# A fused attention recurrence and MLP: order of TensorE's work, masks and turned keys of the later chunks

## The chip, the cores and the metric

The kernel runs on one core of a Trainium2 chip. The metric is device time in microseconds (us) of one execution. The core has five engines with queues of their own, which run beside each other: TensorE (PE: matmuls and transposes; PEld is its loading of weights), VectorE (DVE), ScalarE (ACT), GpSimd (POOL) and SyncE (SP, which here only issues DMAs). Matmuls write into PSUM, everything else lives in SBUF or in DRAM.

## The reference

Two blocks, one behind the other. The first is a gated linear recurrence over 768 positions, for each of 4 batches and 8 heads with 48 elements each; the second an MLP with silu on the 3072 tokens x 384 features that come out of it.

```python
state = zeros(B, H, 48, 48)
for t in range(768):
    state = alpha[:, :, t, :, None] * state + einsum('bhd,bhe->bhde', k[:, :, t], v[:, :, t])
    y[:, :, t] = einsum('bhd,bhde->bhe', q[:, :, t], state)
x = y.transpose(0, 2, 1, 3).reshape(3072, 384)
h = x @ w_in                      # 384 x 2048
out = (h / (1 + exp(-h))) @ w_out # 2048 x 384
```

All is in fp32. The weights come as 64-bit floats and are rounded in the kernel.

## The kernel before

**Chunks.** The 768 positions are cut into 6 chunks of 128 for each of 4 batches: 24 chunks, numbered n = 4 * ci + b (`ci` the place in time, `b` the batch). Heads go in 4 pairs. For a chunk the recurrence becomes a few matmuls. These are its stages:

- `products` (L694): alpha, k and q are turned so that the features lie on partitions; for the first 8 chunks by TensorE with an identity, for the later ones by VectorE (`turned`, L692). A scan along the chunk (L717) gives `u`, the running products of alpha; `least` (L720) is the product over the whole chunk; `kp` is k times `u`.
- `quotient` (L736): a second scan (L746) gives `p`, and q times it (L751) is `qp`, in the same buffer.
- `scores` (L773): kp times qp into two PSUM tiles (`ps_a`), one for each head of the pairs. They are brought into `g` in SBUF with everything above the diagonal set to zero. The state of this batch is then scaled by `least` on ScalarE (L817).
- `values` (L822): `g` times v and qp times the state into PSUM, copied into `xt` (L842), the input of the MLP.
- `states` (L843): k (`kn`, with tokens on partitions) times v, added to the state (L859). The last four chunks have no such stage.

**The MLP in pieces.** Four chunks are a group of 512 tokens, six groups in all. The work of a group is cut into pieces that are woven between the stages of later chunks. `enter_plain` (L888) does the first layer of groups 0 and 1 with plain matmuls and a silu on ScalarE (L900). `enter` (L908) does that of the other groups by a scheme with fewer matmuls and more additions: 20 block products, whose operands are sums of blocks of x (`sums_x`, into `xc`) and of the weights (`sums_w`, into `wx` and `w_in`), and whose results are put together by ScalarE (copies L927, silu L932) and VectorE (L935, L1010). `leave` (L1012) does the second layer in 7 block products of 16 matmul records each (128 x 192), with VectorE's subtractions (L1024), and stores the output tiles `o` (L1033, L1036). `audit` (L653) reads alpha and the weights again and reduces them (L681) for a check of whether the fast way holds; a general way stands behind a branch and is not taken here.

**Order.** A loop over 25 steps with 4 slots runs a chunk's stages, and after each slot `fill` (L1157) releases those pieces whose due time has come; `marks` (L1143) set the due times of the groups. The framework's scheduler may move instructions within an engine's queue as it sees fit, by its own costs, unless an instruction is kept in program order. At step 8 `settle` (L1145) frees the buffers of the first stage and opens those of the second (`late`). From then on every PE instruction is kept in program order, by the small class `pe` that wraps matmul and transpose.

**The later chunks (n >= 8).** In one step: `land` and `scores` of the chunk before, `products`, `quotient`, then `values` and `states` of the chunk before and `flip`. The buffer `p` is one of two in turn. After `flip` the loads of the next chunk are issued on SP's queue: four DMAs each for alpha (`at`), k (`kt`) and q (`qt`), and those of v (`vn`).

- *Mask.* `scores` writes only the part of a chunk that is needed, with the key halves of the second two pairs exchanged. ScalarE copies it into one fixed tile `decayed` (L799 twice, L802 four times a chunk), and GpSimd sets the part above the diagonal to zero in four selects (L806). The part that is never written was set to zero once.
- *Turned keys.* `flip` (L753) and `land` (L765) bring `kp` to `kn`, tokens on partitions: VectorE transposes 32 x 32 blocks (L761), one DMA writes them to DRAM (`flips`, L763), four DMAs read them back in the other order (L771). This is done for chunks 8 to 19.

**Stores.** `o` has three buffers. The stores of the first five groups (40) go out on GpSimd's queue, the last eight on SP's.

Of the kernel before, what the change touches and what calls it, by code (L numbers as in the profile page):

```python
# [355 lines left out]
def quotients(  # L356
# [19 lines left out]
    nc = tc.nc  # L376
    dve, act, gps = nc.vector, nc.scalar, nc.gpsimd

    late = {}

    def in_order(ins):

        return tc.keep_in_program_order(ins) if late else ins

    class pe:
        @staticmethod
        def matmul(*args, **kw):
            in_order(nc.tensor.matmul(*args, **kw))  # L388

        @staticmethod  # L390
        def transpose(*args):
            in_order(nc.tensor.transpose(*args))

    B, H, S, D = q.shape
# [27 lines left out]
    gpool = pool("gpool", 6)  # L422
    opool = pool("opool", 3)
    rpool = pool("rpool")
    dram = pool("dram", 2, bass.MemoryType.DRAM)
    upool = pool("upool")
# [107 lines left out]
    def turns(x, n):  # L534

        return x[(n + 1) % 2]

# [8 lines left out]


    decayed = fix.tile([128, 2 * NP * C], F32, name="g")
    low, high = slice(0, CH), slice(CH, C)
    earlier, later = [(low, 0), (high, 1)], [(low, 1), (high, 0)]  # L550
    ones = consts.tile([128, 1], F32, name="ones")
    gps.memset(ones, 1.0)

# [129 lines left out]

    xts, xcs = {}, {}

# [8 lines left out]
    def products(n):  # L694

        c = ctxs[n]
        sg = seg[0 if late else n % 2]
        ps = {}

        for name in ("a", "k", "q"):  # L700
            if n >= NA:
                if name == "a":
                    turned(c[name], tokens(sg))
                continue
            if n < GB and name != "a":

                at = "kq".index(name)
                ps[name] = (bank(at) if n == 1 else out_bank(at, 512)).rearrange("p (j c) -> p j c", c=C)
            else:
                ps[name] = ps_attn()  # L710
            for j in range(NP):
                pe.transpose(ps[name][:, j, :], c[name][:, 2 * j : 2 * j + 2, :], ident)
            if name == "a":
                act.copy(tokens(sg), ps[name])  # L714
        end = NP * W
        u = upool.tile([128, end + 1], F32, name="u")
        dve.tensor_tensor_scan(u[:, end - 1 :: -1], sg[:, end:0:-1], one[:, end:0:-1],  # L717
                               0.0, ALU.mult, ALU.add)

        dve.tensor_single_scalar(least[:, n, :], u[:, 0:end:W], 2.0**-64, ALU.max)  # L720
        kp = c["kp"] = turns(kps, n) if n < NA else kps[0]
        ut = tokens(u)
        if n >= NA:
            ps["k"] = late["turn"].tile([128, NP, C], F32, name="turn")
            turned(c["k"], ps["k"])
        if n < NA:
            dve.tensor_tensor(kp, ps["k"], ut, ALU.mult)
            quotient(n, sg, ps["q"])
            return
        j = NP // 2  # L730
        dve.tensor_tensor(kp[:, 0:j], ps["k"][:, 0:j], ut[:, 0:j], ALU.mult)
        k, ut = [x[:, j:].rearrange("p j (e c) -> p j e c", e=2) for x in (ps["k"], ut)]
        dve.tensor_tensor(kp[:, j:].rearrange("p j (e c) -> p j e c", e=2)[:, :, ::-1], k, ut, ALU.mult)
        c["sg"] = sg

    def quotient(n, sg=None, q=None):  # L736
# [7 lines left out]
        dve.reciprocal(iv[:, 0:end:W], least[:, n, :])  # L744
        p = turns(qps if n < NA else [qps[0], late["p"]], n)
        dve.tensor_tensor_scan(p[:, 0:end], sg[:, 0:end], iv[:, 0:end], 0.0, ALU.mult, ALU.add)  # L746
# [5 lines left out]

    def flip(n):  # L753

        c = ctxs[n]
        if n < NA or c["ci"] == NCH - 1:
            return
        t = late["turn"].tile([128, NP, C], F32, name="turn").rearrange("p c (j d) -> p c j d", j=NP)  # L760
        dve.transpose(t, c["kp"].rearrange("p j (c i) -> p c j i", i=32))  # L761
        c["flip"] = dram.tile([128, NP * C], F32, name="flips")
        nc.sync.dma_start(c["flip"], t.rearrange("p c j d -> p (c j d)"))  # L763

    def land(n):  # L765
        c = ctxs[n]
        if "flip" in c:
            c["kn"] = work.tile([128, NP, C], F32, name="kn")
            x = c.pop("flip").rearrange("(r d) (i x) -> i d r x", r=4, i=4)
            for i in range(4):  # L770
                nc.sync.dma_start(c["kn"][32 * i : 32 * i + 32], x[i])  # L771

    def scores(n):  # L773
        c = ctxs[n]
        ci, b = c["ci"], c["b"]
        ps = [ps_attn() for _ in range(2)]

        for j in (0, 2, 1, 3):  # L780
            for e in range(2 if n >= NA else 1):
                for u in range(2):
# [4 lines left out]
                              start=True, stop=True)  # L787
        g = decayed.rearrange("p (u j c) -> p u j c", u=2, j=NP)
        swapped = decayed.rearrange("p (o u j c) -> p o u j c", o=2, u=2, j=NP // 2)
        c["g"] = (lambda u, j: g[:, u, j, :]) if n < NA else (  # L790
            lambda u, j: swapped[:, j // 2, u, j % 2, :])
        for u in range(2 if n < NA else 0):
            act.copy(g[:, u], ps[u])
            gps.affine_select(g[:, u], g[:, u], pattern=[[0, NP], [1, C]], compare_op=ALU.is_ge,
                              fill=0.0, base=0, channel_multiplier=-1)
        if n >= NA:
            ps = [x.rearrange("p (o j) c -> p o j c", o=2) for x in ps]
            for u in range(2):
                act.copy(swapped[:, :, u, :, CH:], ps[u][:, :, :, CH:])  # L799
            for r, o in earlier:  # L800
                for u in range(2):
                    act.copy(swapped[r, o, u, :, 0:CH], ps[u][r, o, :, 0:CH])  # L802
            for at, half in ((CH, later), (0, earlier)):
                for r, o in half:
                    x = swapped[r, o].rearrange("p u j c -> p (u j) c")[:, :, at : at + CH]
                    gps.affine_select(x, x, pattern=[[0, NP], [1, CH]],  # L806
                                      compare_op=ALU.is_ge, fill=0.0, base=0, channel_multiplier=-1)
        if n < NA and ci < NCH - 1:
            ps_k = ps_attn()
# [12 lines left out]
    def values(n):  # L822

        c = ctxs[n]
        ci, b, g, qp = c["ci"], c["b"], c.pop("g"), c["qp"]
        vn = c["v"].rearrange("p (j u) d -> p j (u d)", u=2)
        s = st[b].rearrange("p j u e -> p j (u e)")
        py = ps_attn()
        todo = [(3 * j + i, vn[:, j, at : at + 32], g(u, j))
                for j in range(NP) for i, at, u in ((0, 0, 0), (1, 32, 0), (2, 80, 1))]  # L830
        todo += [(3 * j + 1, vn[:, j, 48:80], g(1, j)) for j in range(NP)]
        if ci > 0:
# [10 lines left out]
    def states(n):  # L843
        c = ctxs.pop(n)
        ci, b, vn = c["ci"], c["b"], c["v"]
        if ci < NCH - 1:

            ps = ps_attn()
            for j in range(NP):
                for i in range(4):  # L850
                    r = slice(32 * i, 32 * i + 32)
                    kn = c["kn"][:, j, r] if n < NA else c["kn"][:, i, 32 * j : 32 * j + 32]
                    pe.matmul(ps[r, j, 0:D], lhsT=kn, rhs=vn[:, 2 * j + i // 2, 0:D],
                              start=True, stop=True)
# [14 lines left out]
    def sums_x(grp):  # L869
        xcs[grp] = late["xc"].tile([128, len(SUMS_X), TB], F32, name="xc")  # L870
        for to, sa, a, sb, b in SUMS_X:
            tc.keep_in_program_order(
                combine(block_x(grp, to), sa, block_x(grp, a), sb, block_x(grp, b)))
        yield
# [137 lines left out]
    def leave(grp, h):  # L1012
# [14 lines left out]
        def store(m, c, x, y=None):  # L1027
# [6 lines left out]
            r = b * S + ci * C  # L1034

            (gps if grp < NG - 1 else nc.sync).dma_start(out[r : r + C, c * HO : (c + 1) * HO], o)  # L1036

# [104 lines left out]

    marks = [2 * SLOTS + 2] + [(GB * i + 2 * GB) * SLOTS + 3 for i in range(len(phases))]  # L1143

    def settle():  # L1145
# [4 lines left out]
        quads = pool("quads")  # L1150
        late["p"] = pool("p").tile([128, NP * W + 1], F32, name="p")
        late["quads"] = {name: quads.tile([128, 32 + 4 * NP * D], F32, name=f"{name}t") for name in "akq"}
# [23 lines left out]
    for step in range(STEPS):  # L1176
# [6 lines left out]
        elif step >= NA:  # L1183
            stages = [[(land, 1), (scores, 1)], [(products, 0)], [(quotient, 0)],
                      [(values, 1), (states, 1), (flip, 0)]]
        for slot, group in enumerate(stages):
            for stage, lag in group:
# [6 lines left out]
                if stage is states and n + 1 + NIN < NA:  # L1194
                    load(n + 1 + NIN)
                if stage is flip and n + 1 < NT:
                    load(n + 1)
                if stage is states and n + NV < NT:
                    load_v(n + NV)
            if step * SLOTS + slot == (NA + 1) * SLOTS - 1:  # L1200
                x = decayed.rearrange("p (o i c) -> p o i c", o=2, c=C)
                for r, o in later:
                    gps.memset(x[r, o, :, 0:CH], 0.0)
            fill(step, slot)
# [22 lines left out]
    ps = ps_attn()[0:1, 0, 0:1]  # L1227
    pe.matmul(ps, lhsT=good, rhs=ones, start=True, stop=True)
    dve.tensor_single_scalar(small, ps, 127.5, ALU.is_ge)
# [62 lines left out]
```

## Time and profile before

| | |
|---|---|
| median of 3 runs | 568.21 us (567.66 to 568.32) |
| the profiled execution | 568.32 us, span 566.6 us, mean granted clock of TensorE 0.993 |
| PE busy | 545.6 us (96%) |
| DVE busy | 444.1 us (78%), 801 instructions |
| ACT busy | 207.7 us (37%) |
| POOL busy | 72.6 us (13%) |
| DMA | 70.13 MB, mean 124 GB/s |

The span is that of the instructions on the core; the execution's time holds 1.7 us more. Busy shares are means over stages with different limits, so the profile is read by stage. Its groups of instructions are given as line, engine, operation, out<-in, number, then busy time in all, mean duration in ns, and idle time of the engine just before them with what ended it. The durations of TensorE's matmuls overlap, so that the distance from start to start in a dense stream says what one costs. A wait is told by the engine that waited and by what released it.

The rows that tell what the parts concerned take:

| row | count | busy us | mean ns |
|---|---|---|---|
| L799 ACT copy g<-ps_a, 128x256 | 32 | 10.2 | 369 |
| L802 ACT copy g<-ps_a, 64x128 | 64 | 13.6 | 262 |
| L793 ACT copy g<-ps_a, 128x512 (first 8 chunks) | 16 | 8.6 | 588 |
| L794 POOL select, 128x512 (first 8 chunks) | 16 | 12.5 | 804 |
| L813 ACT copy kn<-ps_a (first 8 chunks) | 8 | 4.8 | 605 |
| L927 ACT copy g<-ps_m, 128x512 | 64 | 36.6 | 588 |
| L935 DVE g<-ps_m,g, 128x512 | 56 | 37.3 | 682 |
| L1036 POOL issue of stores | 40 | 22.1 | 552 |
| L771 SP issue of kn<-flips | 48 | | 430 (median) |
| L763 SP issue of flips | 12 | | 344 (median) |

### The profile page before, as it was taken

How to read it: one execution, taken by the hardware profiler on the slowest of the kernel's cores; microseconds unless marked ns; L12 is line 12 of the kernel's file. 1: busy time of each engine (PE TensorE's matmuls, PEld its weight loads, DVE VectorE, ACT ScalarE, POOL GpSimd, SP SyncE). 2: the span in 40 equal slices, each digit the busy share in tenths (PEclk: the TensorE clock that was granted, in tenths of full speed). 3: DMA queues.
4: the chain of work that ended last, by engine and by line, in shares of the span. 5: the costliest groups of instructions: out<-in, count | busy, mean ns of one | idle time of the engine just before them, and what ended most of it. 6: DMA issues, size and time to landing. Idle time of an engine off the chain costs nothing. (4 is left out here: it accounts for less than half of the span.)

```text
span 566.6 us, 12602 instructions
## 1 busy us (share of the span) xinstructions
PE 545.6 (96%) x5026; PEld 489.6 (86%) x5026; DVE 444.1 (78%) x801; ACT 207.7 (37%) x466; POOL 72.6 (13%) x146
## 2 busy tenths in 40 slices
PE   6999999999979999999999999999999999999995
PEld 4788887998968989889999989998898999997995
DVE  5997879885957799998997988997993776857531
ACT  3565654313312242353341553442462341422100
POOL 3110111221111020210110212110221000001000
PEclk9999999999997999999999999999999999999999
DMA  9999761233542343345546355455432132333010
GB/s 218 251 270 203 203 182 53 63 104 105 144 125 79 109 124 86 101 115 158 161 124 167 113 167 140 128 159 139 120 104 79 53 101 90 112 104 113 29 31 25
DMA packets 99220, 70.13 MB, mean 124 GB/s; under 512 B 56272, under 2 KB 88656, under 8 KB 99152
## 3 DMA queue, kind: packets, MB, share of 16 engines
q1 hardware_dynamic: 97232, 65.30, 43.3%
q0 software_dynamic: 1920, 3.93, 2.0%
q8 instruction: 41, 0.67, 0.5%
q14 instruction: 27, 0.22, 0.1%
HBM read 61.34 MB, written 7.86 MB: 122 GB/s over the span
## 5 line engine op out<-in xcount | busy, mean ns | idle before, releaser
L388 PE MATMUL ps_o<-w_out,g 128*128 128x192 f32 x768 | 134.6, 329 | 1.6 <-DVE o L1033 1.4
L388 PEld LDWEIGHTS ps_o<-w_out,g 128*128 128x128 f32 x768 | 125.4, 190 | 5.5 <-DVE o L1033 2.5
L388 PE MATMUL ps_m<-xt,w_in 128*128 128x256 f32 x480 | 116.6, 390 | 5.0 <-ACT g L900 3.6
L388 PEld LDWEIGHTS ps_m<-xt,w_in 128*128 128x128 f32 x480 | 90.6, 193 | 19.3 <-ACT g L900 3.9
L388 PE MATMUL ps_o<-wt,g 128*128 128x192 f32 x576 | 99.7, 326 | 0.0
L388 PEld LDWEIGHTS ps_o<-wt,g 128*128 128x128 f32 x576 | 95.1, 190 | 1.6 <-issue 0.2
L388 PE MATMUL ps_m<-xc,w_in 128*128 128x256 f32 x288 | 70.8, 382 | 2.0 <-ACT part L927 1.4
L388 PEld LDWEIGHTS ps_m<-xc,w_in 128*128 128x128 f32 x288 | 53.6, 190 | 9.4 <-ACT part L927 1.7
L681 DVE TENSOR_REDUCE seen<-bits 128x1 f32<-128x384 int32 (+2 forms) x65 | 42.5, 688 | 21.3 <-DMA bits<-in_moe_w_out_dram 20.4
L1024 DVE TENSOR_TENSOR g<-g 128x512 f32<-128x512 f32 x72 | 48.5, 689 | 6.1 <-PE ps_o L388 6.1
L932 ACT ACTIVATE g<-g 128x1024 f32<-128x1024 f32 x32 | 33.3, 1056 | 53.1 <-DVE g L935 52.8
L388 PE MATMUL ps_m<-xc,wx 128*128 128x256 f32 x192 | 50.1, 383 | 0.1
L1036 POOL DMA_DIRECT2D out_dram<-o x40 | 22.1, 552 | 219.1 <-DVE o L1033 130.2
L927 ACT COPY g<-ps_m 128x512 f32<-128x512 f32 x64 | 36.6, 588 | 35.4 <-PE ps_m L388 34.9
L806 POOL TENSOR_SCALAR_AFFINE_SELECT g<-g 64x256 f32<-64x256 f32 x64 | 30.5, 477 | 141.3 <-ACT g L799 124.0
L817 ACT ACTIVATE st<-st,least 128x96 f32<-128x96 f32 x80 | 24.3, 365 | 57.4 <-DVE least L720 57.3
L935 DVE TENSOR_TENSOR g<-ps_m,g 128x512 f32<-128x512 f32 x56 | 37.3, 682 | 3.3 <-PE ps_m L388 3.0
L388 PEld LDWEIGHTS ps_m<-xc,wx 128*128 128x128 f32 x192 | 35.1, 190 | 4.6 <-ACT g L927 0.4
L717 DVE TENSOR_TENSOR_SCAN u<-al,one 128x516 f32<-128x516 f32 x24 | 29.5, 1227 | 9.9 <-ACT al L714 9.5
L692 DVE STREAM_TRANSPOSE al<-at 128x512 f32<-128x512 f32 x16 | 17.8, 1111 | 19.3 <-DMA at<-in_alpha_dram 11.9
L900 ACT ACTIVATE g<-ps_m 128x512 f32<-128x512 f32 x32 | 19.0, 595 | 37.5 <-PE ps_m L388 37.4
L746 DVE TENSOR_TENSOR_SCAN p<-al,inv 128x516 f32<-128x516 f32 x24 | 29.6, 1234 | 0.6
(126 smaller groups left out, 617.3 us busy)
## 6 DMA issues: line engine op xcount, KB each, us to landing
bits<-in_moe_w_in_dram SPq DMA_DIRECT2D x24, 512.0 KB, 4.6
bits<-in_moe_w_out_dram SPq DMA_DIRECT2D x32, 384.0 KB, 3.1
at<-in_alpha_dram SPq DMA_DIRECT2D x64, 96.0 KB, 2.5
kt<-in_k_dram SPq DMA_DIRECT2D x64, 96.0 KB, 2.5
qt<-in_q_dram SPq DMA_DIRECT2D x64, 96.0 KB, 2.5
bits<-in_alpha_dram SPq DMA_DIRECT2D x9, 512.0 KB, 3.9
out_dram<-o POOLq DMA_DIRECT2D x40, 96.0 KB, 2.0
flips<-turn SPq DMA_DIRECT2D x12, 256.0 KB, 2.4
```

The lines of the kernel that those rows point to most:

```text
L388: in_order(nc.tensor.matmul(*args, **kw))
L681: dve.tensor_reduce(seen[kind][which][:, i : i + 1], x, axis=AX, op=op, apply_absolute_value=True))
L717: dve.tensor_tensor_scan(u[:, end - 1 :: -1], sg[:, end:0:-1], one[:, end:0:-1], 0.0, ALU.mult, ALU.add)
L746: dve.tensor_tensor_scan(p[:, 0:end], sg[:, 0:end], iv[:, 0:end], 0.0, ALU.mult, ALU.add)
L806: gps.affine_select(x, x, pattern=[[0, NP], [1, CH]], compare_op=ALU.is_ge, fill=0.0, base=0, channel_multiplier=-1)
L817: act.mul(s[:, j], s[:, j], least[:, n, j : j + 1])
L900: act.activation(gts[grp, h, pair][:, i : i + 2, q % 2, :], ps, AF.Silu)
L927: act.copy(to, ps)
L932: act.activation(x, x, AF.Silu)
L935: dve.tensor_tensor(to, a, b, op)
L1024: dve.tensor_tensor(cells(grp, h, pair, *to), cells(grp, h, pair, *x), cells(grp, h, pair, *y), ALU.subtract)
L1036: (gps if grp < NG - 1 else nc.sync).dma_start(out[r : r + C, c * HO : (c + 1) * HO], o)
```

## The change

- The class `pe` goes; TensorE's instructions, and the sums of x on VectorE, are left to the scheduler throughout.
- Masks of the later chunks: two PSUM tiles are blanked by ScalarE (`blank`, behind `quotient`) before the scores are written into parts of them, and VectorE multiplies each whole tile with a mask of ones and zeros into `g`. The mask is built at the start by GpSimd. `g` is a tile of its own for each chunk (one buffer) in place of `decayed`. The masks of the first eight chunks are made as before.
- Turned keys of chunks 8 to 19: by four TensorE transposes with the identity and one ScalarE copy, as in the first eight chunks, in the stage `scores`. `flip`, `land` and the DRAM tile go.
- `p` has one buffer in the later chunks, and `quotient` and `blank` stand behind `values` and `states`. The loads of the next chunk follow `quotient`.
- All stores go out on SP's queue, `o` has two buffers.
- The due times of the groups come one slot earlier.

```diff
-    class pe:
-        @staticmethod
-        def matmul(*args, **kw):
-            in_order(nc.tensor.matmul(*args, **kw))
-        @staticmethod
-        def transpose(*args):
-            in_order(nc.tensor.transpose(*args))
+    pe, dve, act, gps = nc.tensor, nc.vector, nc.scalar, nc.gpsimd
...
-    opool = pool("opool", 3)
+    opool = pool("opool", 2)
...
+    mask = consts.tile([128, 2, C], F32, name="mask")
+    gps.memset(mask, 1.0)
+    for odd in range(2):
+        for e in range(2):
+            m = mask[CH * e : CH * e + CH, odd, :]
+            gps.affine_select(m, m, pattern=[[1, C]], compare_op=ALU.is_ge, fill=0.0,
+                              base=-CH * (e ^ odd), channel_multiplier=-1)
...
-        p = turns(qps if n < NA else [qps[0], late["p"]], n)
+        p = turns(qps, n)
...
-    def flip(n):
...
-        t = late["turn"].tile([128, NP, C], F32, name="turn").rearrange("p c (j d) -> p c j d", j=NP)
-        dve.transpose(t, c["kp"].rearrange("p j (c i) -> p c j i", i=32))
-        c["flip"] = dram.tile([128, NP * C], F32, name="flips")
-        nc.sync.dma_start(c["flip"], t.rearrange("p c j d -> p (c j d)"))
-    def land(n):
...
-            for i in range(4):
-                nc.sync.dma_start(c["kn"][32 * i : 32 * i + 32], x[i])
+    def blank(n):
+        if n < NA:
+            return
+        ps = ctxs[n]["blank"] = [ps_attn() for _ in range(2)]
+        for t in ps:
+            act.activation(t.rearrange("p j c -> p (j c)"), ident[:, 0:1].to_broadcast([128, 4 * C]),
+                           AF.Copy, scale=0.0)
...
-            for u in range(2):
-                act.copy(swapped[:, :, u, :, CH:], ps[u][:, :, :, CH:])
-            for r, o in earlier:
-                for u in range(2):
-                    act.copy(swapped[r, o, u, :, 0:CH], ps[u][r, o, :, 0:CH])
-            for at, half in ((CH, later), (0, earlier)):
-                for r, o in half:
-                    x = swapped[r, o].rearrange("p u j c -> p (u j) c")[:, :, at : at + CH]
-                    gps.affine_select(x, x, pattern=[[0, NP], [1, CH]],
-                                      compare_op=ALU.is_ge, fill=0.0, base=0, channel_multiplier=-1)
-        if n < NA and ci < NCH - 1:
+            m = mask[:, :, None, :]
+            dve.tensor_tensor(g[:, u].rearrange("p (o j) c -> p o j c", o=2),
+                              ps[u].rearrange("p (o j) c -> p o j c", o=2),
+                              m.to_broadcast([128, 2, NP // 2, C]), ALU.mult)
+        if ci < NCH - 1:
             ps_k = ps_attn()
             for j in range(NP):
                 pe.transpose(ps_k[:, j, :], c["kp"][:, j, :], ident)
             c["kn"] = work.tile([128, NP, C], F32, name="kn")
             act.copy(c["kn"], ps_k)
...
-            tc.keep_in_program_order(
-                combine(block_x(grp, to), sa, block_x(grp, a), sb, block_x(grp, b)))
+            combine(block_x(grp, to), sa, block_x(grp, a), sb, block_x(grp, b))
...
-            (gps if grp < NG - 1 else nc.sync).dma_start(out[r : r + C, c * HO : (c + 1) * HO], o)
+            nc.sync.dma_start(out[r : r + C, c * HO : (c + 1) * HO], o)
...
-    marks = [2 * SLOTS + 2] + [(GB * i + 2 * GB) * SLOTS + 3 for i in range(len(phases))]
+    marks = [2 * SLOTS + 2] + [(GB * i + 2 * GB) * SLOTS + 2 for i in range(len(phases))]
...
-            stages = [[(land, 1), (scores, 1)], [(products, 0)], [(quotient, 0)],
-                      [(values, 1), (states, 1), (flip, 0)]]
+            stages = [[(scores, 1)], [(products, 0)], [(values, 1), (states, 1)], [(quotient, 0), (blank, 0)]]
...
-                if stage is flip and n + 1 < NT:
+                if stage is quotient and n + 1 < NT:
                     load(n + 1)
```

## The prediction

> **What bounds the kernel now.** I read the page first: busy shares, then the forty slices.
>
> ```profile
> PE   6999999999979999999999999999999999999995
> DVE  5997879885957799998997988997993776857531
> PEclk9999999999997999999999999999999999999999
> ```
>
> TensorE (PE) is at 9 in all slices but the ends and the twelfth; in the thirteenth its clock was held down. VectorE (DVE), at 78% overall, is the only other engine near full. So the time is TensorE's work plus its waits. The windows show how much idle there is, by stage (length, then PE, PEld, DVE, ACT, POOL busy, the granted clock, DMA):
>
> ```profile
> 60.00:100.00 40.00, 39.19 (x384) 33.28 (x383) 34.15 (x68) 20.83 (x44) 4.85 (x6) 1.00 0.50 138
> 140.00:170.00 30.00, 26.91 (x276) 24.41 (x274) 23.25 (x45) 7.69 (x26) 4.14 (x9) 1.00 0.48 127
> 170.00:185.00 15.00, 14.45 (x163) 12.14 (x164) 10.21 (x21) 3.70 (x12) 2.79 (x6) 0.78 0.32 88
> 185.00:230.00 45.00, 43.63 (x439) 39.45 (x437) 42.01 (x79) 15.83 (x44) 5.82 (x11) 1.00 0.41 110
> ```
>
> From 185 to 510 us PE is busy 322.3 of 325 us (0.84% idle), in program order. From 25 to 140 us, nearly all in the scheduler's order, it is busy 113.7 of 115 (1.2% idle). Between them lies the one large loss. The waits of PE (total, times, longest):
>
> ```profile
> PE ps_m L388 <- ACT g L900: 3.6, 1, 3.6
> PE ps_o L388 <- DVE o L1033: 1.4, 2, 1.3
> PE ps_m L388 <- ACT part L927: 1.4, 1, 1.4
> PE ps_m L388 <- ACT g L927: 0.6, 1, 0.6
> ```
>
> Timelines of SP, DVE, ACT and PE (start, duration, instruction, idle before) trace the 3.6 us to its root:
>
> ```profile
> 160.61 0.40 SPq L499 DMA_DIRECT2D vn<-in_v_dram  x1
> 162.41 1.07 SPq L482 DMA_DIRECT2D at<-in_alpha_dram  x2
> 165.56 1.11 DVE L692 STREAM_TRANSPOSE al<-at 128x512 f32<-128x512 f32 x1 [6.11 <-DMA at<-in_alpha_dram]
> 169.23 0.64 ACT L817 ACTIVATE st<-st,least 128x96 f32<-128x96 f32 x2 [8.78 <-DVE least L720]
> 170.55 5.49 PE L388 MATMUL ps_m<-xt,w_in 128*128 128x256 f32 x12 [3.64 <-ACT g L900]
> ```
>
> Chunk 11's alpha was issued late on SP, so its transpose and scan (to `least`) were late. The scaling of the state on ScalarE (L817) waited 8.78 us for `least`, and the silu (L900) that frees PE's bank was queued behind it. Then 12 matmuls took 5.41 us to the next start, where four elsewhere take 0.86 (12: 2.6), at a granted clock of 0.50 from 170 to 176. With some 0.2 on the scores times v that follow, the slow clock cost 3.0 us. Stall and clock: 6.6 us.
>
> **The change, part by part.** The rows used (busy, mean ns, idle before):
>
> ```profile
> L392 PE MATMUL ps_a<-ident,kp 128*128 128x128 f32 x32 | 5.3, 287 | 0.0
> L806 POOL TENSOR_SCALAR_AFFINE_SELECT g<-g 64x256 f32<-64x256 f32 x64 | 30.5, 477 | 141.3 <-ACT g L799 124.0 <-ACT g L802 14.1
> L761 DVE STREAM_TRANSPOSE turn<-kp 128x512 f32<-128x512 f32 x12 | 8.5, 707 | 0.2
> ```
>
> *Turning kp on PE.* Twelve chunks (8 to 19) get four transposes each, 48 in all, on the engine that bounds. The early chunks' row gives 5.3/32 = 0.166 us each, 8.0 in all. In a dense stream like transposes of four start 0.44 us after one another (an at 82.15, kn 82.59, qn 83.03 us), and up to 0.49 at 96 us: 5.3 to 5.9. I take 12 x 0.49 = **+5.9** (5.3 to 8.0), since these groups stand in a dense stream. What they replace, the DVE transpose (8.5 us), 12 stores to DRAM and 48 loads on SP (some 0.43 us of issue each, 25 with the stores), was beside PE. Their 12 copies out of PSUM (605 ns, L813: 7.3 us) fall on ScalarE, 37% busy, with four to ten us of matmuls before the first user.
>
> The Trainium skill ("TensorE: Matmul & The Clock Gate", Part 4) puts a 128x128 PE transpose, of bf16, at some 275 ns inside a kernel; by it the 48 would cost 13.2 us, as an estimate, and the sum would be 7.3 us higher. The trace's starts say less than half, and decide.
>
> *Masks of late chunks.* Off: ScalarE's copies (32 x 369 + 64 x 262 ns = 28.6 by durations, 23.8 by busy time) and GpSimd's 30.5 us. On: 32 ScalarE activations that blank two PSUM tiles, 128x512, nearest row L927 at 588 ns (18.8 us; 0.37 to 1.06 us each by L799 and L932, 12 to 34), and 32 DVE products 128x512 from PSUM, nearest row L935 at 682 ns (21.8 us). A chunk's mask chain falls from six copies and four selects (1.8 + 1.9 = 3.7 us by durations) to two products (1.4 us); but it moves onto the fuller engine. DVE in all: +21.8 - 8.5 = **+13.3** busy, to 457. ScalarE: -23.8 + 18.8 + 7.3, about +2. None of this is on PE's path by itself: it is hidden by the MLP's pieces between scores and values (2.6 us each, and the built order keeps 8 to 11 us of them). If that cover is gone, all 13.3 land on PE.
>
> *Stores and queues.* 40 stores of `o` go from GpSimd's queue (22.1 us) to SP's, at about 0.5 us of issue each. SP loses 60 issues and gains 40. `o` has two buffers: at 2.6 us per product a buffer is wanted again after 5.2, against 0.5 + 2.0 to land; 2.7 us to spare. Behind a store that waits for `o`, SP queues the loads of q, k, alpha and v. They are issued a chunk (20 us) ahead: price nothing, up to the one late load above.
>
> *Order.* PE no longer follows program order. Quotient goes behind values and states, and `p` has one buffer: the scan of the next `p` must wait for the values before it. From there to the scores DVE needs 1.23 (L746) + 0.69 + what stands between, 3 to 7.5 us, under 8 to 11 of fill: 1 to 2 us to spare where it is tightest.
>
> In the order of the changed kernel as built, chunk 11's state scaling stands behind the silu that stalled, not ahead of it. `least` is then due 10.5 us after the states of chunk 9 by the rows' durations, and wanted at 15.8. So I take the stall and its slow clock away: **-6.6** (0 if it stays or comes back).
>
> The skill (same page, Part 1) says an idle of about a 3.4 us window halves the clock until PE has been busy as long. The trace agrees that 3.64 us did it and 1.37 did not, but the slow clock lasted 6.8 us. By the rule any new wait past 3.4 us would cost its length and 1.7 more; by the trace, 3.0 more.
>
> *New waits.* The scheduler's order idles 1.2% where program order idles 0.84%: 0.36% of 325 us = +1.2. Where groups enter at 185 to 230 us, DVE was busy 42.0 of 45; 2.2 chunks there (20.3 us apart, by the loads of kn) add 0.66 each, so 43.5 of 45, and its queue is as good as full. I charge four chunks of that group one DVE instruction each (0.69): +2.8. Together **+4.0**; bounds -3.3 (the waits of 1.37, 0.64 and 1.25 us go as well and none comes) and +13.3 (all that DVE gains). I stay near the lower end, since PE waited for DVE in only 0.5 us at ps_m.
>
> **The sum** is against the profiled execution: 568.32 us (span 566.6, 1.7 around it), 0.1 above the median 568.21. 568.3 + 5.9 - 6.6 + 4.0 = 571.6; I say **571.5**, slower by 0.6%. A measurement of this kernel tells 0.2%, 1.1 us, from no change.
>
> **The rivals.**
> A, *the stall stays or comes back*: a load late behind a store on SP, or a group entry that starves PE past 3.6 us. For it: DVE waited 11.9 us in all for alpha, five times; the margins are 1 to 2 us. Against: 60 issues less on SP, and the silu is ahead. 571.6 + 6.6 = **578**.
> B, *faster*: the scheduler fills PE wherever it can, so that the stall goes and no wait replaces it. For it: it put the silu ahead, and 6.6 exceeds the transposes' 5.9. Against: 1.2% against 0.84% idle. With no new wait 568.3 + 5.9 - 6.6 = 567.6; with the three other waits gone too, at 5.3 for the transposes, 563.7; middle **565.7**. It decides once waits sum to less than -0.4.
> C, *DVE becomes the bound*: its 13.3 us show on PE. For it: 42 of 45 at the group entry. Against: 36 of 40 later, and 28 from 430 us. 568.3 + 5.9 - 6.6 + 13.3 = **581**.
> D, *no change to be told*: new waits of -0.4 to 1.8 us, about **568.3**.
>
> **How the numbers follow.** Forecast (569.4 to 575) 0.50, A 0.22, C 0.05, D 0.11, B 0.12. Hence faster 0.12, same 0.11, slower 0.77. The range is 566.5 to 580: it leaves out the better part of B and the worst of C, under 2 in 10. The forecast's own range is 569.4 to 575.
>
> **What would show it.** In the changed profile: transposes of kp x80 at the old mean; DVE near 457, POOL near 20 us; no 9-to-7 in the clock's slices; PE's waits for DVE at `g`, `p` or `kp` some 4 us more, mostly from 185 to 230 us. The wait for L900 near 3.6 us and a 7 in the clock mean A; DVE at 9 through 230 to 400 us with PE at 8 means C. I would be wrong most of all if the PSUM tiles, blanked early and held until the scores, made values or states wait: three buffers serve five uses a chunk, and I priced that at nothing because each is read by ScalarE or DVE well before its turn comes.

## The result and the profile after

The changed kernel takes 561.19 us (median of 4 runs, 560.85 to 561.29), the kernel before 567.93 us beside it (567.44 to 568.32, 4 runs): a ratio of 0.9881, 95% interval 0.9864 to 0.9898. It is 1.2% faster, where 571.5 us, slower by 0.6%, was forecast; the time lies below the forecast's range too.

The slices of the changed kernel, to be set beside those of before:

```profile
PE   5999999999999999999999999999999999999996
DVE  5887789956998799986998897899895885857731
POOL 5110000300000000000000000000000000000000
PEclk9899999999999999999999999999999999999999
```

The 7 in the clock's thirteenth slice is gone, and TensorE is at 9 everywhere but at the ends. (There is an 8 in the clock near the start: 3.4 us at half clock from 14.3 us, behind a stall of 1.71 us that ended at 13.86.) The windows, with the same columns as before:

```profile
140.00:170.00 30.00, 30.00 (x360) 27.70 (x349) 28.79 (x54) 9.83 (x23) 0.00 (x0) 1.00 0.39 97
170.00:185.00 15.00, 15.00 (x186) 13.55 (x185) 13.30 (x27) 4.52 (x10) 0.00 (x0) 1.00 0.45 115
185.00:230.00 45.00, 45.00 (x452) 41.16 (x451) 40.79 (x84) 16.12 (x34) 0.00 (x0) 1.00 0.32 84
510.00:540.00 30.00, 30.00 (x180) 29.08 (x179) 18.87 (x42) 4.33 (x7) 0.00 (x0) 1.00 0.24 73
```

By these rows TensorE never stands still in the stretch from 140 to 230 us, where it idled 3.1 + 0.6 + 1.4 us before, nor from 510 to 540, where it was busy 28.52 of 30 before. From 185 to 510 us it is busy 324.3 of 325 us: 0.2% idle, where 0.84% was. The waits of TensorE that are left, without those at the start:

```profile
PE ps_m L860 <- ACT xt L807: 0.8, 3, 0.3
PE ps_a L817 <- DVE kp L711: 0.5, 1, 0.5
PE ps_m L884 <- DVE g L898: 0.4, 1, 0.4
PE ps_a L776 <- DVE st L823: 0.4, 1, 0.4
PE ps_m L884 <- ACT g L890: 0.3, 1, 0.3
```

All the waits that the prediction listed are gone in this execution, and none took their place. What was added cost this (group, busy, mean ns, idle before):

```profile
L770 DVE TENSOR_TENSOR g<-ps_a,mask 128x512 f32<-128x512 f32 x32 | 20.5, 683 | 3.5 <-PE ps_a L759 3.3
L743 ACT ACTIVATE ps_a<-ident 128x512 f32<-128x512 f32 x32 | 19.0, 599 | 0.4
L776 PE MATMUL ps_a<-ident,kp 128*128 128x128 f32 x80 | 13.1, 286 | 0.4 <-DVE st L823 0.4
```

**Where the time went.** TensorE's matmuls can be counted by the distance from one start to the next. A dense stream has the same pace in both kernels (0.163 us for a record of 192 columns, 0.216 for one of 256). Whatever a distance is longer than the pace is lost, be it a wait or the slow clock. This count was made from both traces; its rows are rounded, and their level hangs on the pace taken for the small records:

| stage (us from the start) | lost before | lost after |
|---|---|---|
| 0 to 25 | 7.2 | 8.7 |
| 25 to 100 | 3.4 | 3.6 |
| 100 to 185 | 9.4 | 1.9 |
| 185 to 250 | 4.7 | 1.7 |
| 250 to 470 | 5.9 | 4.6 |
| 470 to the end | 3.0 | 0.3 |
| sum | 33.8 | 20.8 |

Lost time falls by 13.0 us, work grows by the transposes' 5.9: -7.1, and 0.4 comes off behind the last matmul, which makes the 7.5 us between the spans (566.6 and 559.1). The 7.1 can be read without the table: the last matmul starts at 560.5 us before and at 553.4 after.

### The profile page after: what moved, and what is told of

Read it like the earlier page. It is cut to its first block, busy times and chain, and to the rows that moved or that the text cites. A ratio compares the mean times of both kernels' runs of the same rounds, so it can differ in the third digit from the quotient of the medians.

```text
span 559.1 us, 12435 instructions
## 1 busy us (share of the span) xinstructions
PE 543.4 (97%) x5074; PEld 492.6 (88%) x5074; DVE 448.1 (80%) x821; ACT 208.9 (37%) x414; POOL 20.8 (4%) x44
## 4 chain that ended last, share of the span: by engine, by line
PE 79%; DVE 12%; DMA 3%; ACT 2%; SPq 1%; issue 1%; POOL 0%; DVEq 0%; ACTq 0%
PE ps_o L982 35%; PE ps_m L884 21%; PE ps_m L860 11%; PE ps_a L802 6%; PE ps_a L759 3%; PE ps_a L776 2%; DMA qn<-in_q_dram 1%; DVE g L898 1%; DMA bits<-in_moe_w_in_dram 1%; DVE u L701 1%; PE ps_a L817 1%; DVE p L730 1%; DVE seen L665 1%; SPq L456 1%; DVE w_out L626 1%
## 5 line engine op out<-in xcount | busy, mean ns | idle before, releaser
L860 PE MATMUL ps_m<-xt,w_in 128*128 128x256 f32 x384 | 88.3, 382 | 0.8 <-ACT xt L807 0.8
L860 PEld LDWEIGHTS ps_m<-xt,w_in 128*128 128x128 f32 x384 | 71.1, 190 | 10.6 <-ACT xt L807 1.2
L802 PE MATMUL ps_a<-g,vn 128*32 128x128 f32 x768 | 27.9, 281 | 1.8 <-POOL g L766 1.7
L802 PEld LDWEIGHTS ps_a<-g,vn 128*32 128x32 f32 x768 | 20.4, 111 | 9.1 <-issue 5.6
L890 ACT COPY part<-ps_m 128x512 f32<-128x512 f32 x32 | 18.6, 582 | 21.8 <-PE ps_m L884 17.6
```

The costliest lines, as they stand in the source:

```text
L802: pe.matmul(py[32 * at : 32 * at + 32, t, :], lhsT=w, rhs=x, start=(i < 4), stop=(i >= len(todo) - 4), skip_group_check=True)
L860: pe.matmul(ps[:, e, :], lhsT=w_in[:, t, (f + e) * 128 : (f + e + 1) * 128], rhs=xt[:, t, :], start=(t == 0), stop=(t == NKT - 1))
L890: act.copy(to, ps)
```

## The experiments

Three theories went in. 1: program order made the waits, and the scheduler's order took them away. 2: the 60 DMAs of the turned keys stood in SP's queue ahead of loads, and their going took the waits away. 3: the masks had stood in ScalarE's queue ahead of what frees TensorE's banks. The runs were made in five groups, each with the kernel before beside it, and ratios are against that. Its time was 568.0, 570.8, 572.2, 572.0 and 573.1 us in the five groups, so times are compared within a group, and ratios across groups. Even the ratio has limits there: the changed kernel had 0.9881 in the result and 0.9822 in the fourth group. Differences of some 0.6% between groups show nothing.

**One part at a time.** In the kernel before, order alone:

```diff
-        return tc.keep_in_program_order(ins) if late else ins
+        return ins
...
-            tc.keep_in_program_order(combine(...))
+            combine(...)
```

> The kernel before with one thing changed: TensorE and the sums of x are left to the scheduler throughout. Theory 1 (order: program order made the waits): the waits of about 9.6 us and the slow clock of 3.0 go, with no transposes to pay: 555 to 558. Theory 2 (SP's queue: the flips' 60 DMAs delay the loads) and theory 3 (masks in ScalarE's queue hold up what frees TensorE's banks): the stall stays, 565 to 569.

Measured 569.57 us, ratio 1.0013 (0.999 to 1.0037): no gain. The stall of 3.6 us went, but TensorE waited 5.1 us for `p` in place of it, and after a stall of 1.80 us the clock was half for 3.4 us. Theory 1 alone falls.

In the changed kernel, the class `pe` and the order of the sums put back (the same lines the other way):

> The changed kernel with TensorE and the sums of x in program order again from the eighth chunk on. Theory 1: the waits come back, 568 to 574. Theories 2 and 3: 561 to 563, since SP's queue and ScalarE's stay as changed.

Measured 568.56 us, ratio 1.001 (0.9986 to 1.0035). Here an order does cost, some 7 us, the whole gain: TensorE waited twice, 4.0 us in all, for `xc`, and after each wait the clock was half for 3.4 us (from 282.8 and from 371.5 us). Which of the two orders it is was asked below.

In the kernel before, TensorE's transposes for the turned keys, all else left:

```diff
-        if n < NA and ci < NCH - 1:
+        if ci < NCH - 1:
             ps_k = ps_attn()
...
     def flip(n):
-        if n < NA or c["ci"] == NCH - 1:
+        if True:
             return
...
-                    kn = c["kn"][:, j, r] if n < NA else c["kn"][:, i, 32 * j : 32 * j + 32]
+                    kn = c["kn"][:, j, r]
```

> The kernel before with the turned keys by TensorE transposes, all else as before. Theories 1 and 3: 567.9 + 5.9 = 573.8, the stall of 3.6 us and the slow clock stay. Theory 2: they go with SP's 60 DMAs, 567 or less.

Measured 563.67 us, ratio 0.9917 (0.9893 to 0.9941): faster, with TensorE in program order and the old masks, and with 5.9 us more for TensorE to do. Theory 2 holds so far, and theory 3 is not needed for this gain; whether it is the queue or something else in the turned keys is asked below. VectorE's waits for alpha's DMA fell from 11.9 to 1.4 us (kernel before, then this run):

```profile
DVE al L692 <- DMA at<-in_alpha_dram: 11.9, 5, 6.1
```

```profile
DVE al L692 <- DMA at<-in_alpha_dram: 1.4, 1, 1.4
```

The reverse, in the changed kernel: `flip`, `land` and their DMAs on SP put back in place of the transposes. `flip` stands ahead of `quotient` here, where it stood behind it in the kernel before.

> The changed kernel with the turned keys of chunks 8 to 19 by VectorE and DRAM again, in place of 48 transposes on TensorE. Theories 1 and 3: 12 groups x 0.49 us less work on TensorE and no new wait, 561.2 - 5.9 = 555.3. Theory 2: the late loads come back with the 60 DMAs on SP, 560 to 568.

Measured 581.03 us, ratio 1.0237 (1.0191 to 1.0282): 20 us slower than the changed kernel, though TensorE has 5.9 less to do. The wait of TensorE that grew most:

```profile
PE ps_a L780 <- DVE p L736: 4.9, 11, 1.2
```

The scores wait for `p` eleven times; VectorE turns `kp` ahead of the product into `p` (206.22 and 214.28 us for one chunk), where in the kernel before it did so behind it (218.62 after 217.43). The direction was theory 2's, but the size beyond all that was expected: these waits are 4.9 of the 20 us, and the run does not share out the rest between the queue, the place of `flip` and the longer way to `kn`.

**What in the turned keys costs?** Three runs: transposes on TensorE used for `kn`, with VectorE's transposes kept beside them unused (first), and with the 60 DMAs on SP kept too, the read-back going to DRAM (second); and the kernel before with its DMAs on GpSimd's queue (third).

The second run, in `land`, on top of the transposes (`kd` is a tile in DRAM):

```diff
-            c["kn"] = work.tile([128, NP, C], F32, name="kn")
+            c["kd"] = dram.tile([128, NP, C], F32, name="kd")
...
-                nc.sync.dma_start(c["kn"][32 * i : 32 * i + 32], x[i])
+                nc.sync.dma_start(c["kd"][32 * i : 32 * i + 32], x[i])
```

The third, against the kernel before:

```diff
-        nc.sync.dma_start(c["flip"], t.rearrange("p c j d -> p (c j d)"))
+        gps.dma_start(c["flip"], t.rearrange("p c j d -> p (c j d)"))
...
-                nc.sync.dma_start(c["kn"][32 * i : 32 * i + 32], x[i])
+                gps.dma_start(c["kn"][32 * i : 32 * i + 32], x[i])
```

> As the run before it, without the DMAs: TensorE transposes for kn and VectorE's 12 transposes of 0.71 us kept, unused. If SP's queue makes the waits: 563 to 565. If it is VectorE's 8.5 us: 568 to 575.

Measured 565.13 us, ratio 0.9905 (0.9877 to 0.9933). VectorE's 8.5 us cost nothing.

> The kernel before with TensorE transposes for kn, and beside them VectorE's transposes and all 60 DMAs kept on SP (the read-back goes to DRAM and nobody uses it). If load on SP and VectorE makes the waits: 572 to 575, that is the time before plus 5.9. If waiting for kn itself makes them: 563 to 565, as with the transposes alone.

Measured 574.98 us, ratio 1.0089 (1.006 to 1.0118). The DMAs on SP, which nobody uses, cost 9.9 us (574.98 - 565.13). They reach TensorE as waits for `p`, and the clock was half for 3.4 us twice (from 181.5 and 201.9 us):

```profile
PE ps_a L388 <- DVE p L751: 5.9, 3, 2.7
```

> The kernel before with the 60 DMAs of the turned keys on GpSimd's queue in place of SP's, TensorE's order unchanged. If SP's queue makes the waits: 563.7 - 5.9 = 558. If GpSimd's selects now wait behind these DMAs: 565 to 575.

Measured 564.21 us, ratio 0.9895 (0.9871 to 0.992). The same transfers on another queue: 6.6 us faster than the kernel before beside it (570.84). So it is their place in SP's queue, not the transfers as such. In this kernel the other queue does as well as the transposes (564.21 against 565.13), though it leaves TensorE 5.9 us less to do. It is not the 558 that was hoped for: TensorE's waits for VectorE's `o` grew from 1.4 to 3.1 us, and VectorE waited 4.6 us for the buffer that the store to DRAM reads.

What SP's queue waited for shows how (kernel before; then the run with DMAs that nobody uses; total, times, longest):

```profile
SPq L763 <- DVE turn L761: 60.7, 9, 11.4
```

```profile
SPq L763 <- DVE turn L761: 35.6, 7, 8.7
```

The store of a chunk's turned keys (L763) waits at the head of SP's queue until VectorE has made `kp` and transposed it. The loads of the next chunk's alpha stand behind it. The timeline of SP in the kernel before, ahead of the 3.6 us stall:

```profile
148.78 2.56 SPq L771 DMA_DIRECT2D kn<-flips  x4
151.44 0.38 SPq L482 DMA_DIRECT2D at<-in_alpha_dram  x1
158.73 0.34 SPq L763 DMA_DIRECT2D flips<-turn  x1
159.12 1.39 SPq L482 DMA_DIRECT2D at<-in_alpha_dram  x1
```

SP issued the first part of chunk 11's alpha at 151.44 us, then stood at chunk 10's store until 158.73, and only then came to the other three parts. In the changed kernel VectorE hardly waits for the loads:

```profile
DVE al L676 <- DMA kt<-in_k_dram: 1.7, 1, 1.7
DVE al L676 <- DMA at<-in_alpha_dram: 0.7, 1, 0.7
```

Before, it was 11.9 us for alpha, 3.8 for k and 3.5 for v ahead of the same instruction. But standing at the head of the queue is not yet a cost. In the changed kernel SP stands longer than that for the stores of `o`, which are now in its queue, with loads behind them:

```profile
SPq L998 <- DVE o L996: 73.0, 33, 5.6
SPq L998 <- ACT o L994: 29.9, 11, 7.5
```

These are 102.9 us in more and shorter pieces, and the loads still come in time. A run below, with these stores on GpSimd's queue, is no faster.

In the changed kernel, the DMAs of `flip` and `land` on GpSimd's queue:

> The changed kernel with the keys turned by VectorE and DRAM, as in the earlier run of that kind, but its 60 DMAs on GpSimd's queue, which is nearly empty there. If SP's queue (loads behind the flips) made the waits: near 555, at least 15 us below the 581 of the run with them on SP. If the longer way to kn or VectorE's transposes made them: 575 to 582.

Measured 572.94 us, ratio 1.0042 (1.0019 to 1.0065). That is in neither of the expected ranges. The queue is worth 2.0% (from 1.0237), but 1.6% over the changed kernel (0.9881 in the result) stays: TensorE waits 5.3 us for `p` and 5.4 for `g` of the MLP. The way through DRAM costs in a second manner there, and the runs don't say which part of it does.

**The rest of the gain.** Four runs of one group, the changed kernel among them.

> The changed kernel itself, beside the three that follow on one chip: ratio 0.985 to 0.990 against the kernel before.

Measured 562.08 us, ratio 0.9822 (0.9801 to 0.9842): lower than expected, and than in the result. The changed kernel took nearly the same time as there (561.19), the kernel before 4 us more.

> The kernel before with TensorE transposes for kn, again, beside the changed kernel: if the transposes are the whole gain, within 1 us of the changed kernel; if masks and order give the rest, 2 to 4 us above it.

Measured 565.93 us, ratio 0.9894 (0.9873 to 0.9915): 6.1 of the 9.9 us that this group shows between the kernels come from the turned keys.

The same with the changed masks (`mask`, `blank` and two products as in the change; two buffers for `o` to make room):

> The run before it with the changed masks as well (two tiles blanked by ScalarE, two products on VectorE; two buffers for o to make room), TensorE in program order. If VectorE's 13 us of more work, beside 28 of ScalarE and 30 of GpSimd less, cost nothing: within 1 us of the transposes alone. If they land on TensorE's path: 4 to 13 us above. If the shorter chain helps: 1 to 3 us below.

Measured 563.91 us, ratio 0.986 (0.9835 to 0.9885): 2.0 us below the run without, though the intervals overlap. That the masks cost nothing is shown; that they gain is likely. The 1.8 us from here to the changed kernel stand for all that is left (orders, `p`, due times, stores) and are not shared out.

The changed kernel with the sums of x alone in program order:

> The changed kernel with the sums of x alone in program order on VectorE, TensorE free. If the sums' place made the two waits of 2 us for xc and the slow clock: 5 to 8 us above the changed kernel. If it takes both orders, or TensorE's: 0 to 2 us above.

Measured 565.90 us, ratio 0.9889 (0.9865 to 0.9913): 3.8 us above the changed kernel, between the two expectations: the waits came, the slow clock did not. The waits of TensorE and the place of one:

```profile
PE ps_m L885 <- DVE xc L562: 3.3, 2, 1.7
```

```profile
281.73 1.97 PE L885 MATMUL ps_m<-xc,w_in 128*128 128x256 f32 x8 [1.60 <-DVE xc L562]
```

A group's first products wait for the sums, which stand late in VectorE's queue: the first starts at 281.2 us here, at 275.2 in the changed kernel. The next three runs are of the third group (the kernel before at 572.18), which has no run of the changed kernel. The other order alone, in the changed kernel:

> The changed kernel with TensorE alone in program order, the sums of x free. If the two waits of 2 us for xc in the run with both came from the sums' place on VectorE: they go, ratio 0.988 to 0.992. If TensorE's own order makes them: they stay, 0.998 to 1.003.

Measured 563.47 us, ratio 0.9849 (0.9829 to 0.9869). No wait for `xc` is left. The ratio is below the range that was expected for this; against 0.9822 for the changed kernel TensorE's order costs nothing that can be told across groups.

The stores on GpSimd's queue and three buffers for `o`, in the changed kernel:

> The changed kernel with the 40 stores on GpSimd's queue again and three buffers for o. If SP's queue is still tight: up to 3 us faster than the changed kernel (ratio 0.983 to 0.987). If it is relieved by the 60 DMAs that went: 0.987 to 0.990.

Measured 562.09 us, ratio 0.9828 (0.9805 to 0.985): below both ranges, as the changed kernel itself was. Against its 0.9822, queue of the stores and number of buffers make no difference that can be told.

The kernel before with transposes, both orders left to the scheduler:

> The kernel before with TensorE transposes for kn, and TensorE and the sums of x left to the scheduler as well. If the order is worth something only once SP's DMAs are gone: 1 to 3 us under the run with the transposes alone (ratio 0.986 to 0.990 against its 0.992). If the order is worth it only with the changed stages and masks: 0.992 or more.

Measured 564.96 us, ratio 0.9877 (0.9853 to 0.9901): not to be told from the transposes alone (0.9917 and 0.9894 in other groups).

**Is there better than both?** Three more arrangements that leave the turned keys to DRAM, on GpSimd's queue. In the kernel before, with the stores on SP as well:

> The kernel before with the 60 DMAs of the turned keys on GpSimd's queue and the 40 stores on SP's. If GpSimd's queue held up the turned keys and the stores: 0.980 to 0.986, faster than the changed kernel. If 40 stores are enough to delay SP's loads: 0.990 or more.

Measured 567.67 us, ratio 0.9921 (0.99 to 0.9941), no better than with the stores on GpSimd's queue (0.9895 in another group).

With the changed masks and the sums left to the scheduler, stores on GpSimd's queue:

> The kernel before with three edits: the 60 DMAs of the turned keys on GpSimd's queue, the changed masks (two buffers for o), the sums of x left to the scheduler. If SP's queue, the masks and the sums' place are all that cost: on the earlier chip 564.2 less 2 for the masks and up to 3.8 for the sums, 558 to 562, ratio 0.978 to 0.985, at or below the changed kernel's 0.982. If the way through DRAM itself is too long: 0.988 or more.

Measured 565.93 us, ratio 0.9881 (0.9862 to 0.99).

```profile
PE ps_a L388 <- ACT ps_a L781: 2.5, 4, 1.1
```

```profile
DVE turn L694 <- DMA flips<-turn: 5.6, 5, 1.9
```

TensorE waits for the blanked tiles, and VectorE for a buffer that a store to DRAM still reads: what the transposes cost may come back as these new waits.

And with TensorE left to the scheduler too:

> The run before it with TensorE left to the scheduler too. If the scheduler places scores and values by a kn that it takes to be earlier than it is, as in the changed kernel with these DMAs: 5 us or more above the run before it. If TensorE's order doesn't matter: within 1.5 us of it.

Measured 566.34 us, ratio 0.9883 (0.9864 to 0.9902): as the run before it. No run's time is below the changed kernel's 561.2 and 562.1 us, though that was not run in this last group.

## Why the prediction was wrong, point by point

- *The transposes, +5.9*: right. In all 12 groups the distance from the first transpose to what follows is 0.49 us, though the row's mean is 286 ns. The Trainium skill's price ("TensorE: Matmul & The Clock Gate", Part 4: some 275 ns for a 128x128 transpose, of bf16) would have made it 13.2 us, as an estimate, over twice as much.
- *The stall and its slow clock, -6.6*: right in size. From 100 to 185 us the loss fell by 7.5. I gave as ground the place of a state's scaling behind a silu. That place is enough: with order alone in the kernel before, the silu runs at 166.01 us, the scaling at 171.78, and the stall is gone, though alpha is as late as ever. It isn't needed: with transposes alone the scaling still runs ahead of the same silu (161.95 and 166.94 us), and the stall is gone since alpha's transpose starts at 159.35 in place of 165.56. The changed kernel has the silu first (166.75, scaling at 168.71) and no store of turned keys ahead of alpha's load; which of the two cured it there is open.
- *Masks*: priced at nothing unless the cover went, and the cover held. VectorE's products take 21.9 us and the 8.5 went, as worked out. Yet the durations of all its instructions grew by 7.9 us only (487.9 to 495.7), since other rows got shorter, and its busy time by 4.0 (444.1 to 448.1), since instructions overlap more; ScalarE's by 1.2 where 2 were said, GpSimd's is 20.8 where 20 were. Blanked PSUM tiles that hold up values or states, named as the likeliest way to be wrong, did not show in the changed kernel: the one wait of TensorE there for what frees such a tile is 0.4 us (L776).
- *New waits, +4.0*: this is the step that failed. Forecast was that the scheduler's order and VectorE's fuller queue add waits; waits went instead. The term is -6.8: the spans differ by -7.5, and 5.9 - 6.6 accounts for -0.7. By the table's rounded rows, the loss fell by 7.0 from 185 us on, by 0.9 more than stall and clock from 100 to 185, by 0.4 behind the last matmul; it rose by 1.7 in the first 100 us. I had read 1.2% of idle between 25 and 140 us as the scheduler's order and 0.84% later as program order. These were two stages with other work, and the order is not what sets their idle: taking it away gained nothing in the kernel before, and in the changed one most of what putting it back costs comes by the sums' place and the slow clock behind their waits.
- *"Price nothing"* for SP's queue was the root. I had counted 60 issues that go and 40 that come, by the time that an issue takes. What counted is what an issue waits for: the store of the turned keys stood 60.7 us at the head of the queue, nine times, with loads behind it that VectorE then waited for. I had the view of VectorE's 21.5 us of waits for alpha, k and v and charged them to one stall only. For the 40 stores the price of nothing was right, though SP stands 102.9 us for them.
- *Bounds*: the end of -3.3 took in three single waits above 0.6 us. The lost time beside them was as large: from 185 us on, dense matmuls of 192 and 256 columns lost 6.6 us before and 3.4 after in distances 0.1 to 0.6 us over the pace.
- Of the rivals, B, "faster", had the sign, with 0.12; its lowest sum, 563.7, is still above the time. So the sign was partly luck: its ground, the scheduler's order, brought nothing by itself in the kernel before. A's late load is the very mechanism, but the change cures it. C did not come about: VectorE is at 40.8 of 45 from 185 to 230 us, less than before.

## What to carry to other kernels

Price a DMA in a queue by what it waits for and by what stands behind it, and not by its issue. A transfer that depends on a late result does harm ahead of loads that are wanted soon; where the loads behind it still come in time, as behind the stores of the changed kernel, it costs nothing that these runs show. So ask when the loads behind must land. Work on the bounding engine can be cheaper than a detour that leaves that engine free, if the detour's waits reach it; in the kernel before, moving the detour to another queue did as well. Before idle is put down to an order, take the order away alone: here that was worth nothing by itself, while the same order put back into the changed kernel took the whole gain.

## What was not expected of the hardware

A stall well under 3.4 us can bring the slow clock, and its length alone does not decide. In the changed kernel with both orders back, TensorE stood 1.93 us, and the granted clock was half for 3.4 us from 282.8 us on. The line of the stall, and the windows after it (granted clock third from the end):

```profile
281.97 2.96 PE L387 MATMUL ps_m<-xc,w_in 128*128 128x256 f32 x8 [1.93 <-DVE xc L577]
```

```profile
282.00:284.00 2.00, 2.00 (x7) 1.66 (x8) 2.00 (x6) 0.58 (x1) 0.00 (x0) 0.70 0.72 231
284.00:287.00 3.00, 3.00 (x12) 2.52 (x11) 1.31 (x4) 1.06 (x2) 0.00 (x0) 0.63 0.07 26
287.00:290.00 3.00, 3.00 (x46) 2.69 (x46) 2.86 (x5) 0.43 (x2) 0.00 (x0) 1.00 0.00 0
```

The stall of 1.60 us with the sums alone in order brought none, nor did 1.37 us in the kernel before; after 3.64 us there the clock was slow for 6.8 us. But no length divides the two. The stall of 1.71 us near the start of the changed kernel brought the slow clock. One of 1.85 us in the changed kernel with the DMAs of the turned keys on GpSimd's queue brought none (granted clock 1.00 from 163 to 168 us):

```profile
164.70 1.02 PE L780 MATMUL ps_a<-p,kp 48*64 48x128 f32 x32 [1.85 <-DVE p L736]
```

Where a stall lies seems to count beside its length: the two slow stretches with both orders back begin 88.75 us apart, 26 times 3.413 us, and no run varies the place alone. Which stalls bring the slow clock is in so far luck. The Trainium skill ("TensorE: Matmul & The Clock Gate", Part 1) tells of a window of some 3.4 us; the lengths, 3.4 and 6.8, are one and two of these, but that an idle must fill the window is not what these runs show.
